# LayerNorm at the start of a spectral block plus MLP kernel: four groups of four token tiles instead of five groups of two and four, first scaling on Pool, first tables issued from the ACT queue

## The chip, the cores and the metric

The kernel runs on one core of a Trainium2 chip. The metric is device time in microseconds (us) of one execution; the kernel before takes 502.8 us. The profiled span is about 2 us shorter than the device time of the same execution.

Names: PE is the matrix engine, DVE the vector engine, ACT the scalar engine, Pool the GPSIMD engine, SP the engine that here issues most DMA transfers.

## The reference

The change touches only the first LayerNorm, without scale and offset, whose result goes into a two-dimensional Fourier transform.

```python
def _layernorm(x, axis=-1, eps=1e-5):
    m = jnp.mean(x, axis=axis, keepdims=True)
    v = jnp.var(x, axis=axis, keepdims=True)
    return (x - m) / jnp.sqrt(v + eps)

def _A_ref(x, w_r, w_i):                     # x: 1 x 2048 x 576, bf16
    X = rfft2(x.astype(float32)) * (w_r + 1j * w_i)
    return irfft2(X, s=(2048, 576)).astype(bfloat16)

h  = x + _A_ref(_layernorm(x), A_w_r, A_w_i)
h2 = h + ((gelu(LN(h) @ w_gate) * (LN(h) @ w_up)) @ w_down)     # the MLP
```

## The kernel before

The 2048 tokens lie in 16 tiles of 128. The sequence transform's first stage multiplies a tile (as weights) by a table of 128 columns. LayerNorm's factor 1/sqrt(var + eps) is one number per token, so the kernel scales the *table* with it (`ATS = ATB * RS1`) and never the tile. Variances are worked out for a group of tiles at once, and the five groups run as a pipeline:

1. statistics of each tile: on DVE two `bn_stats` and one `bn_aggr` (`ln1_tile`), or, for the tiles in `ACT_TILES`, sum and sum of squares on ACT (`act_sum`, `act_sq`) and two one-column steps on DVE;
2. square root on ACT, reciprocal on DVE;
3. table scaling, on DVE (four instructions of 128 columns) or Pool (one of 512);
4. matmuls on PE, five outputs k of each group;
5. evictions, that is copies, of the five results from PSUM (the memory that PE writes to) into `U` on ACT or DVE (`a_evs`).

When all of `U` is there, the forward DFT over the columns starts (`st_D`, "PS<-FT,U"), then the spectral stage (`st_B`, "PS<-CUS,BT").

```python
    P.op(POOL, lambda g: g.memset(EPT[:, :], EPS), w=["EPT"])
    # ... more memsets on Pool
    x_load(0, 0, 2)            # all on the SP queue; x_load(i, c0, c1) = tiles c0..c1-1
    x_load(1, 2, 4)
    atb_load(0, 0, 4)          # table columns of tiles 0 to 3
    x_load(2, 4, 8)
    atb_load(1, 4, 8)
    x_load(3, 8, 12)
    x_load(4, 12, 16)
    atb_load(2, 8, 16)
    # [cut]
    GROUPS = ((0, 2), (2, 4), (4, 8), (8, 12), (12, 16))
    ACT_TILES = (1, 3, 7, 11, 13)

    def ln1_var(i):
        c0, c1 = GROUPS[i]
        for c in range(c0, c1):
            if c in ACT_TILES:         # TM = sum^2 / D^2: one column, both inputs in SBUF
                P.op(DVE, lambda v, c=c: v.scalar_tensor_tensor(TM[:, 0, c:c + 1], SA[:, 0, c:c + 1], 1.0 / (D * D), SA[:, 0, c:c + 1],
                                                                op0=ALU.mult, op1=ALU.mult), r=[("SA0", c)], w=[("TM", c)])
            else:
                P.op(DVE, lambda v, c=c: v.bn_aggr(MV1[:, c, :], ST1[:, c, :, :]), r=[...], w=[("MV1", c)])
        for c in range(c0, c1):
            if c in ACT_TILES:         # variance = squares / D - TM
                P.op(DVE, lambda v, c=c: v.scalar_tensor_tensor(MV1[:, c, 1:2], SA[:, 1, c:c + 1], 1.0 / D, TM[:, 0, c:c + 1],
                                                                op0=ALU.mult, op1=ALU.subtract), r=[...], w=[("MV1", c)])

    def ln1_scale(i, eng):
        c0, c1 = GROUPS[i]
        if eng == POOL:
            P.op(POOL, lambda g, c0=c0, c1=c1: g.tensor_tensor(ATS[:, c0:c1, :], ATB[:, c0:c1, :],
                 RS1[:, c0:c1].unsqueeze(2).to_broadcast([128, c1 - c0, 128]), op=ALU.mult), r=[...], w=[...])
        else:
            for c in range(c0, c1):
                P.op(DVE, lambda v, c=c: v.tensor_scalar(ATS[:, c, :], ATB[:, c, :], RS1[:, c:c + 1], None, op0=ALU.mult), r=[...], w=[...])

    def idle_mm(n, i):     # n matmuls of zeros, to keep PE busy while it has nothing to do
        ...
    # the order of issue, group by group [cut to its start]
    idle_mm(11, 0)
    act_sum(1); act_sq(1)
    ln1_tile(0); ln1_tile(2)
    act_sum(3)
    ln1_var(0); ln1_sqrt(0)
    act_sq(3)
    ln1_rs(0); ln1_scale(0, DVE); a_mms(0)
    ln1_var(1); ln1_sqrt(1)
    a_evs(0, ACT, (0, 1, 2, 3, 4))
    ln1_rs(1); ln1_scale(1, DVE)
    idle_mm(2, 1)
    a_mms(1)
    ln1_tile(4); ln1_tile(5); ln1_tile(6)
    # [cut: groups 2, 3 and 4]
```

## Time and profile before

| | value |
|---|---|
| device time, median of 3 | 502.81 us (502.74 to 503.13) |
| profiled span | 501.2 us |
| PE busy, whole span | 98% |
| start of tile 4's statistics on DVE | 8.22 us |
| first forward-DFT matmul | 20.17 us |

First, lines of the page of the kernel before: the engines' busy times, and the clock granted to PE in 40 slices of 12.5 us.

```profile
PE 492.9 (98%) x4319; PEld 299.5 (60%) x4319; DVE 182.5 (36%) x391; ACT 158.4 (32%) x296; POOL 39.8 (8%) x49
...
PE   7999999999999999999999999999999999999998
...
PEclk9899999999999999999999999999999999999999
```

PE has idle time to lose only in the first slice (7 tenths) and in the last (8 tenths, which the change does not touch), and a lower clock mainly in the second (8 tenths). The change lies in these two slices, and it can gain or lose only by moving the moment at which the forward DFT starts. Next the chain of waits of the kernel before, that is, the work that ended last, followed back. The columns are start, duration and what ran.

```profile
2.12 6.08 DMA XO<-in_A_x_dram
...
8.22 2.26 DVE ST L440 x6
...
17.65 0.58 DVE ATS L472 x3
18.23 1.80 DVE U L505 x3
20.04 0.14 issue
20.17 2.55 PE PS L600 x18
22.72 0.52 PE PS L626 x6
```

It starts with the x transfer for tiles 4 to 7, issued at 2.12 and landed at 8.2. From then on DVE works almost without a gap to its last eviction, and the forward DFT starts at 20.17.

DVE scales tables for group 1 until about 8.1, so an x that lands earlier than that would find DVE busy. And the one-column step of tile 13 (line 446, at 16.04) takes 0.11 us.

Last, two rows of the busy-by-window view of the kernel before: busy time and instruction count per engine, the mean granted clock, and the DMA share.

```profile
core 0: us, PE busy (x) PEld busy (x) DVE busy (x) ACT busy (x) POOL busy (x), PEclk, DMA share, GB/s
...
13.70:17.10 3.40, 3.40 (x21) 2.12 (x22) 3.40 (x15) 3.40 (x10) 1.04 (x1) 0.50 1.10 228
```

PE ran at half clock from 13.7 to 17.1, and ACT was as busy as DVE there.

### The profile page before, as it was taken

How to read it: one execution, taken by the hardware profiler on the slowest of the kernel's cores; microseconds unless marked ns; L12 is line 12 of the kernel's file. 1: busy time of each engine (PE TensorE's matmuls, PEld its weight loads, DVE VectorE, ACT ScalarE, POOL GpSimd, SP SyncE). 2: the span in 40 equal slices, each digit the busy share in tenths (PEclk: the TensorE clock that was granted, in tenths of full speed). 3: DMA queues.
4: the chain of work that ended last, by engine and by line, in shares of the span. 5: the costliest groups of instructions: out<-in, count | busy, mean ns of one | idle time of the engine just before them, and what ended most of it. 6: DMA issues, size and time to landing. Idle time of an engine off the chain costs nothing.

```text
span 501.2 us, 9972 instructions
## 1 busy us (share of the span) xinstructions
PE 492.9 (98%) x4319; PEld 299.5 (60%) x4319; DVE 182.5 (36%) x391; ACT 158.4 (32%) x296; POOL 39.8 (8%) x49
## 2 busy tenths in 40 slices
PE   7999999999999999999999999999999999999998
PEld 2687674444457764444477744444677544444775
DVE  5899663344331114433311044433201233333111
ACT  7888766653220012332300023232100123233000
POOL 3645290000000000000000000000000000000000
PEclk9899999999999999999999999999999999999999
DMA  8769989001100000100000001100000000000000
GB/s 280 168 203 327 313 288 319 2 7 25 26 1 19 18 13 20 22 14 1 2 12 13 19 18 21 24 2 1 1 18 19 13 1 1 1 2 1 13 19 19
DMA packets 25948, 28.64 MB, mean 57 GB/s; under 512 B 11568, under 2 KB 19888, under 8 KB 25776
## 3 DMA queue, kind: packets, MB, share of 16 engines
q1 hardware_dynamic: 23328, 17.39, 12.1%
q0 software_dynamic: 2576, 10.62, 6.3%
q8 instruction: 34, 0.56, 0.5%
q14 instruction: 10, 0.08, 0.1%
HBM read 23.66 MB, written 2.36 MB: 52 GB/s over the span
## 4 chain that ended last, share of the span: by engine, by line
PE 90%; DVE 7%; issue 1%; DMA 1%; SPq 0%; ACT 0%; DVEq 0%
PE PS L861 56%; PE PS L884 28%; PE PS L723 3%; DVE TP L635 2%; PE PS L762 2%; DVE ST L440 1%; DMA XO<-in_A_x_dram 1%; DVE ZS L640 1%; DVE CUS L613 1%; PE PS L600 1%; DVE U L505 0%; SPq L206 0%; PE PS L807 0%; PE PS L654 0%; DVE CUS L610 0%
## 5 line engine op out<-in xcount | busy, mean ns | idle before, releaser
L861 PE MATMUL PS<-HT,WGU 64*128 64x512 bf16 x2592 | 281.9, 376 | 0.0
L861 PEld LDWEIGHTS PS<-HT,WGU 64*128 64x128 bf16 x2592 | 137.9, 94 | 142.8 <-issue 1.2
L873 ACT ACTIVATE GL<-PS 128x512 bf16<-128x512 f32 x144 | 85.9, 597 | 289.3 <-PE PS L861 288.5
L874 DVE TENSOR_TENSOR AT<-GL,PS 128x512 bf16<-128x512 bf16 x144 | 98.9, 688 | 174.2 <-PE PS L861 172.5
L884 PE MATMUL PS<-WD,AT 128*128 128x288 bf16 (+2 forms) x1152 | 141.8, 286 | 0.0
L884 PEld LDWEIGHTS PS<-WD,AT 128*128 128x128 bf16 x1152 | 111.0, 98 | 31.5 <-issue 1.7
L887 DVE TENSOR_TENSOR OS<-PS,XO 128x288 bf16<-128x288 f32 (+2 forms) x32 | 14.6, 458 | 125.8 <-PE PS L884 125.8
L674 POOL TENSOR_SCALAR WS<-WS 128x290 bf16<-128x290 bf16 x16 | 15.9, 996 | 9.6 <-DMA WS<-in_A_w_i_dram 5.9
L765 DVE SCALAR_TENSOR_TENSOR XO<-PS,XO 128x576 bf16<-128x576 f32 x16 | 12.1, 756 | 8.4 <-PE PS L762 8.4
L600 PE MATMUL PS<-FT,U 128*128 128x290 bf16 x96 | 14.4, 287 | 0.4 <-DVE U L505 0.4
L723 PE MATMUL PS<-DT,V 128*128 128x289 bf16 x96 | 14.6, 287 | 0.2 <-DVE V L660 0.2
L635 DVE TENSOR_TENSOR TP<-YS,WS 128x580 bf16<-128x580 bf16 (+2 forms) x34 | 14.1, 453 | 0.3 <-issue 0.3
L654 PE MATMUL PS<-VT,ZS 128*128 128x256 bf16 x96 | 13.1, 272 | 1.0 <-DVE ZS L640 1.0
L665 ACT ACTIVATE V<-PS 128x768 bf16<-128x768 f32 x15 | 12.2, 810 | 1.2 <-PE PS L654 1.0
L629 ACT ACTIVATE YS<-PS 128x578 bf16<-128x578 f32 x16 | 10.5, 654 | 3.3 <-PE PS L626 2.9
L732 ACT ACTIVATE GS<-PS 128x578 bf16<-128x578 f32 x15 | 9.8, 654 | 4.2 <-PE PS L723 4.1
L723 PEld LDWEIGHTS PS<-DT,V 128*128 128x128 bf16 x96 | 8.9, 97 | 3.5 <-issue 0.4
L600 PEld LDWEIGHTS PS<-FT,U 128*128 128x128 bf16 x96 | 9.2, 98 | 2.9 <-issue 0.6
L753 ACT ACTIVATE OS<-XO 128x576 bf16<-128x576 bf16 x16 | 10.8, 674 | 0.0
L626 PE MATMUL PS<-CUS,BT 128*128 128x289 bf16 (+2 forms) x96 | 10.7, 247 | 0.0
L762 PE MATMUL PS<-GS,IT 128*128 128x288 bf16 x64 | 10.5, 285 | 0.0
L483 PE MATMUL PS<-ZD 128*128 128x512 bf16 x24 | 9.1, 537 | 1.3 <-POOL ZD L377 1.3
(58 smaller groups left out, 156.6 us busy)
## 6 DMA issues: line engine op xcount, KB each, us to landing
WD<-in_B_w_down_dram POOLq DMA_DIRECT2D x9, 576.0 KB, 8.4
WGU<-in_B_w_up_dram SPq DMA_DIRECT2D x4, 1152.0 KB, 9.7
WGU<-in_B_w_gate_dram POOLq DMA_DIRECT2D x4, 1152.0 KB, 10.3
out_dram<-OS SPq DMA_DIRECT2D x30, 72.0 KB, 1.6
XO<-in_A_x_dram SPq DMA_DIRECT2D x3, 576.0 KB, 7.6
IT<-c_itab SPq DMA_DIRECT2D x1, 1024.0 KB, 7.0
HT<-HN SPq DMA_TRANSPOSE x60, 2.4
XO<-in_A_x_dram SPq DMA_DIRECT2D x2, 288.0 KB, 3.1
```

What stands on the lines that cost most here:

```text
L600: P.op(PE, lambda t, b=b, o=o, dt=dt, us=us, g=g: t.matmul(bank(b, 0, 128, 0, 2 * HK), U[:, us, g, :, :], FT[:, o, dt, :], start=(dt == 0) ...
L635: P.op(DVE, lambda v: v.tensor_tensor(TP[:, sl, t_, :, q0:q1], YS[:, sl, :, q0:q1], WS[:, g, w_, q0:q1], op=ALU.mult), r=[("Y", sl), ("Wn" ...
L654: P.op(PE, lambda t, b=b, o=o, c=c, zp=zp, sl=sl, sp_=sp_: t.matmul(bank(b, 0, 128, o, o + 256), ZS[:, sl, zp, 128 * c:128 * c + 128], VT[ ...
L665: P.op(ACT, lambda a, g=g, src=src: a.activation(V[:, :, :, g, :], src, ACTF.Copy), r=[("PS", bs[0]), ("PS", bs[2]), "Vfree"], w=[("V", g, ...
L674: P.op(POOL, lambda v, g=GORD[i]: v.tensor_scalar(WS[:, g, 0, :], WS[:, g, 2, :], -1.0, None, op0=ALU.mult), r=[k for k in wkeys[0 if 1 <= ...
L723: P.op(PE, lambda t, b=b, h=h, i=i, kt=kt, c=c: t.matmul(bank(b, 0, 128, 0, K2), V[:, kt, c, :, :], DT[:, 3 * h + i, 0:K2], start=(i == 0) ...
L762: P.op(PE, lambda t, b=b, h=h, i=i, c=c, rhs=rhs: t.matmul(bank(b, 0, 128, 0, 288), IT[:, h * i, c, :], rhs, start=(i == 0), stop=(i == 1) ...
L861: op = P.op(PE, lambda t, h0=h0, kt=kt, wt=wt, f=f, b=b, HT=HT, s=(half == 0 and j in (0, 5)), e=(half == 1 and j in (3, 8)): t.matmul(ban ...
L873: P.op(ACT, lambda a, s2=s2, b0=b0: a.activation(GL[:, s2, :], bank(b0), ACTF.Gelu_apprx_tanh), r=[("PS", b0)], w=[("GL", s2)])
L874: P.op(DVE, lambda v, s2=s2, b0=b0, f=f: v.tensor_tensor(AT[:, f, :], GL[:, s2, :], bank(b0 + 1), op=ALU.mult), r=[("GL", s2), ("PS", b0 + ...
L884: P.op(PE, lambda t, b=b, d0=d0, d1=d1, f=f, p=p: t.matmul(bank(b, 0, 128, 0, d1 - d0), AT[:, f, 128 * p:128 * p + 128], WD[:, f, d0:d1], ...
L887: P.op(DVE, lambda v, b=b, d0=d0, d1=d1, p=p, c=c: v.tensor_tensor(OS[:, p % 2, d0:d1], bank(b, 0, 128, 0, d1 - d0), XO[:, c, d0:d1], op=A ...
```

## The change

The intent: two small groups cost DVE two rounds of small steps and four table scalings before tile 4 can start. One group of four tiles, three on DVE and one on ACT, with its table scaled by Pool, should let DVE start on tile 4 as soon as x arrives; and with the first table loads moved to ACT's queue, x should be issued earlier. A tiny multiply on Pool is meant to bring the loading of Pool's library forward to where nothing waits for it.

```diff
     P.op(POOL, lambda g: g.memset(EPT[:, :], EPS), w=["EPT"])
+    P.op(POOL, lambda g: g.tensor_tensor(RS2[:, 0:1], EPT[:, :], EPT[:, :], op=ALU.mult), r=["EPT"], w=[("V2", 0)])
 ...
     x_load(0, 0, 2)
     x_load(1, 2, 4)
-    atb_load(0, 0, 4)
     x_load(2, 4, 8)
-    atb_load(1, 4, 8)
     x_load(3, 8, 12)
     x_load(4, 12, 16)
     atb_load(2, 8, 16)
 ...
-    GROUPS = ((0, 2), (2, 4), (4, 8), (8, 12), (12, 16))
-    ACT_TILES = (1, 3, 7, 11, 13)
+    GROUPS = ((0, 4), (4, 8), (8, 12), (12, 16))
+    ACT_TILES = (1, 7, 11, 13)
 ...
-    idle_mm(11, 0)
+    atb_load(0, 0, 4, ACT)
+    atb_load(1, 4, 8, ACT)
+    idle_mm(17, 0)
 ...            # the new order; group 0 scaled by Pool, group 3 by DVE. Its part from group 1 on:
+    ln1_rs(1)
+    ln1_scale(1, POOL)
+    idle_mm(5, 1)
+    a_mms(1)
 ...
+    ln1_var(2)
+    a_evs(1, ACT, (0,))
+    ln1_sqrt(2)
+    act_sum(13)
+    act_sq(13)
+    ln1_tile(14)
+    ln1_rs(2)
+    ln1_scale(2, POOL)
+    ln1_tile(15)
+    a_evs(1, ACT, (1,))
+    ln1_var(3)
+    a_evs(1, DVE, (4,))
+    ln1_sqrt(3)
+    a_evs(1, ACT, (2, 3))
+    idle_mm(4, 2)
+    a_mms(2)
```

More of the change, by code (lines that the diff above doesn't have):

```diff
@@ L385, in x_load, with atb_load @@
         P.dma(SP, XO[:, c0:c1, 0:D], xv[:, c0:c1, :], f"x{i}", w=[("X", c) for c in range(c0, c1)])
-    def atb_load(i, c0, c1):
-        P.dma(SP, ATB[:, c0:c1, :], tabs[:, c0:c1, :], f"atb{i}", w=[("ATB", c) for c in range(c0, c1)])
+    def atb_load(i, c0, c1, eng=SP):
+        P.dma(eng, ATB[:, c0:c1, :], tabs[:, c0:c1, :], f"atb{i}", w=[("ATB", c) for c in range(c0, c1)])
     x_load(0, 0, 2)
     x_load(1, 2, 4)
-    atb_load(0, 0, 4)
     x_load(2, 4, 8)
-    atb_load(1, 4, 8)
     x_load(3, 8, 12)
@@ L522, in _build @@
     ln1_tile(2)
-    act_sum(3)
+    ln1_tile(3)
     ln1_var(0)
     ln1_sqrt(0)
-    act_sq(3)
     ln1_rs(0)
-    ln1_scale(0, DVE)
+    ln1_scale(0, POOL)
     a_mms(0)
-    ln1_var(1)
-    ln1_sqrt(1)
-    a_evs(0, ACT, (0, 1, 2, 3, 4))
-    ln1_rs(1)
-    ln1_scale(1, DVE)
-    idle_mm(2, 1)
-    a_mms(1)
     ln1_tile(4)
@@ L541, in _build @@
     act_sq(7)
-    a_evs(1, ACT, (0, 1))
+    a_evs(0, ACT, (0, 1, 2))
+    ln1_var(1)
+    ln1_sqrt(1)
+    a_evs(0, ACT, (3, 4))
+    ln1_tile(8)
+    ln1_rs(1)
+    ln1_scale(1, POOL)
+    idle_mm(5, 1)
+    a_mms(1)
+    ln1_tile(9)
+    ln1_tile(10)
+    ln1_tile(12)
+    act_sum(11)
+    act_sq(11)
     ln1_var(2)
+    a_evs(1, ACT, (0,))
     ln1_sqrt(2)
-    a_evs(1, ACT, (2, 3, 4))
-    ln1_tile(8)
+    act_sum(13)
+    act_sq(13)
+    ln1_tile(14)
     ln1_rs(2)
     ln1_scale(2, POOL)
-    idle_mm(7, 2)
-    a_mms(2)
-    act_sum(11)
-    act_sq(11)
-    ln1_tile(9)
-    ln1_tile(10)
-    act_sum(13)
-    ln1_var(3)
-    ln1_sqrt(3)
-    act_sq(13)
-    ln1_tile(12)
-    ln1_rs(3)
-    ln1_scale(3, POOL)
-    ln1_tile(14)
-    a_evs(2, ACT, (0, 1, 2))
-    ln1_tile(15)
-    ln1_var(4)
-    a_evs(2, DVE, (4,))
-    ln1_sqrt(4)
-    ln1_rs(4)
-    ln1_scale(4, DVE)
-    a_evs(2, ACT, (3,))
-    idle_mm(4, 3)
-    a_mms(3)
-    a_evs(3, ACT, (0,))
-    a_evs(3, DVE, (1,))
-    a_evs(3, ACT, (2,))
-    a_evs(3, DVE, (3,))
-    a_evs(3, ACT, (4,))
-    a_mms(4)
-    a_evs(4, DVE, (0,))
-    a_evs(4, ACT, (1,))
-    a_evs(4, ACT, (2,))
-    a_evs(4, DVE, (3,))
-    a_evs(4, ACT, (4,))
+    ln1_tile(15)
[5 more added lines that the diff above has]
+    idle_mm(4, 2)
+    a_mms(2)
+    ln1_rs(3)
+    ln1_scale(3, DVE)
+    a_evs(2, ACT, (0, 1))
+    a_evs(2, DVE, (2, 3))
+    a_evs(2, ACT, (4,))
+    a_mms(3)
+    a_evs(3, ACT, (0, 1))
+    a_evs(3, DVE, (2,))
+    a_evs(3, ACT, (3,))
+    a_evs(3, DVE, (4,))
     uk = [[("U", i, k) for i in range(len(GROUPS))] + ["Uz"] for k in range(5)]
```

## The prediction

> **What bounds the kernel now.** The page gives PE 98% of the 501.2 us span, but the change touches only the first 20 us. The chain of waits there runs: x transfer for tiles 4 to 7 (lands at 8.2), then DVE without a gap (statistics, reciprocals, table scaling, evictions) until the first forward-DFT matmul (L600) at 20.17. After that the spectral stage is DVE-bound (32.2 of 33.5 us busy, busy-by-window view) and then PE-bound, so a shift of the 20.17 start should reach the end about one to one. ACT is just as full: the timeline shows it busy from 12.04 to 20.47 without a gap over 0.2 us.
>
> **What the change removes, adds, moves.**
> - Groups of two tiles (0-1, 2-3) become one of four. Before tile 4 can start, DVE drops four table scalings (0.17 us apart) and one set of small variance steps, and gains two statistics (0.37 each). DVE should be done with group 0 at 7.0 rather than 8.14. After tile 4 its work is nearly the same (scalings 4, evictions 5, statistics alike).
> - ACT loses one tile's two sums (1.35 us), but before 8 us, where it waits for x anyway. After 8.7 us it has ten-plus evictions of 512 columns (0.48 us apart) in place of five of 256 (0.26): some 1 us more.
> - The two small table loads leave the SP queue, so x for tiles 4-7 is issued at about 1.65 instead of 2.11 and x for 8-15 0.9 earlier. The Trainium skill (DMA: Bandwidth & Descriptors, "Issuing engines are not separate DMA queues") says that only issue time is saved; the trace agrees that the engines are near saturation from 5 us. I expect tiles 4-7 at 7.3 to 8.0, and the first table at about 6.5.
> - The first scaling goes to Pool: one 1.04 us instruction, result at about 8.2, so matmuls of group 0 from 8.3.
> - The tiny Pool multiply pulls the Pool library configuration (in the trace at 4.43 us, behind the memsets, hidden in a wait of 7.3 us) to 1.45 us, ahead of memsets worth 3.0 us. The skill (GPSIMD Engine Reference, "Instruction dispatch") gives about 6 us for a first call after such a load. This trace bounds it only from above: under 7.3 us.
>
> **Sum.** Laying the measured durations in program order gives (my estimate): with a load under 3 us, last eviction 0.0 to 0.7 us earlier; break-even near 3.3 us; with 6 us Pool runs configuration to 7.4, memsets to 10.9, the scaling at 11, group-0 evictions on ACT at 12.5, and the second square root, behind those in ACT's order, at 14 instead of 11.05. DVE then sits at the reciprocal for some 2.7 us, and the end moves by 2.5 to 2.9 us. I give the long load somewhat over half. The weight loads that wait for the second memset are delayed about 1 us, with about 4 us of slack.
>
> **Predicted: 504.0 us**, range 502.0 to 506.0. Faster by over 2%: 0.003; within 2%: 0.992; slower: 0.005.
>
> **What would show it.** Right: a gap on Pool of several us after 1.45 before the tiny multiply; the first scaling at 10 or later; a DVE wait of over 1 us at the second reciprocal; L600 starting at 21.5 to 23. Wrong: scaling at 7.2 to 7.6, group-0 matmuls at 8.3, no DVE gap, L600 at 19.5 to 20.2 and a time of 502.2. The half-speed clock seen at 13.7 to 17.1 should vanish in that case.
>
> **What would make it wrong.** A short or already resident library; x landing later because two queues interleave; ACT rather than DVE ending last; slack downstream that swallows the shift.

## More of the kernel before

On the timeline of DVE in the kernel before one can see what it did just before tile 4. The number in brackets would be an idle time and what ended it; there is none at 8.22.

```profile
7.52 0.17 DVE L462 RECIPROCAL RS<-RS 128x2 f32<-128x2 f32 x1 [0.36 <-ACT RS L457]
7.72 0.42 DVE L472 TENSOR_SCALAR ATS<-ATB,RS 128x128 bf16<-128x128 bf16 x2
8.22 2.26 DVE L440 BATCH_NORM_STATS2 ST<-XO 128x6 f32<-128x288 bf16 x6
...
16.04 0.11 DVE L446 SCALAR_TENSOR_TENSOR TM<-SA 128x1 f32<-128x1 f32 x1
```

## The result, and the profile after

| | before | after |
|---|---|---|
| device time, median of 4 | 502.77 us (502.59 to 503.13) | 503.30 us (502.65 to 503.51) |
| ratio after/before | | 1.0007, 95% interval 0.9990 to 1.0025 |
| profiled span | 501.2 us | 501.2 us |

The outputs are correct. A ratio is the mean time of one kernel's fast runs over that of the other's fast runs of the same rounds, so it is not quite the ratio of the medians quoted. The two kernels take the same time within what these runs can tell. This is within the predicted range, but the sum that led to 504.0 did not come about, as the profile shows. The page of the kernel after hardly differs from the page before.

```profile
PE 492.8 (98%) x4320; PEld 299.5 (60%) x4321; DVE 182.3 (36%) x387; ACT 156.4 (31%) x286; POOL 40.7 (8%) x51
...
PEclk9899999999999999999999999999999999999999
```

**The library load.** The timeline of Pool in the kernel after:

```profile
1.30 0.10 POOL L378 MEMSET EPT<- 128x1 f32 x1
1.49 0.19 POOL L379 TENSOR_TENSOR RS<-EPT 128x1 f32<-128x1 f32 x1
...
7.24 1.04 POOL L466 TENSOR_TENSOR ATS<-ATB,RS 128x512 bf16<-128x512 bf16 x1 [2.48 <-DVE RS L461]
11.77 1.04 POOL L466 TENSOR_TENSOR ATS<-ATB,RS 128x512 bf16<-128x512 bf16 x1 [3.49 <-DVE RS L461]
15.25 1.04 POOL L466 TENSOR_TENSOR ATS<-ATB,RS 128x512 bf16<-128x512 bf16 x1 [2.45 <-DVE RS L461]
```

There is no gap of several us before the tiny multiply. The first real scaling starts at 7.24 and was waiting for DVE's reciprocal, which ended at 7.1. The raw instruction records (not a view of the profile; start in us, duration in ns) also name the configuration instructions, which the timeline leaves out:

```
after:   1.342  11 MODIFY_POOL_CONFIG
         1.372  11 MODIFY_POOL_CONFIG
         1.483 192 TENSOR_TENSOR RS<-EPT
before:  4.425  11 MODIFY_POOL_CONFIG
         4.455  11 MODIFY_POOL_CONFIG
         4.514 7346 EVENT_SEMAPHORE        (a wait)
        11.965 1037 TENSOR_TENSOR ATS<-ATB,RS
```

From the second configuration record to the first multiply it is 0.11 us. Before, the same would have been hidden in a wait of 7.35 us, which is why that trace could only bound it from above.

**The start of tile 4.** The timeline of DVE in the kernel after:

```profile
6.92 0.18 DVE L461 RECIPROCAL RS<-RS 128x4 f32<-128x4 f32 x1 [0.36 <-ACT RS L456]
8.02 2.26 DVE L439 BATCH_NORM_STATS2 ST<-XO 128x6 f32<-128x288 bf16 x6 [0.92 <-DMA XO<-in_A_x_dram]
...
15.84 0.47 DVE L445 SCALAR_TENSOR_TENSOR TM<-SA 128x1 f32<-128x1 f32 x1
```

DVE is free at 7.1, as planned, and then waits 0.92 us for the x of tiles 4 to 7, although its transfer was issued 0.48 us earlier than before (1.64 against 2.12). Note also the last line: the one-column step takes 0.47 us in place of 0.11.

**The end of the stage.** The chain of waits of the kernel after:

```profile
1.64 6.36 DMA XO<-in_A_x_dram
...
8.02 2.26 DVE ST L439 x6
...
15.92 0.39 DVE TM L445
...
16.61 0.30 ACT RS L456
16.91 3.85 ACT U L506 x8
20.75 0.05 issue
20.80 2.04 PE PS L591 x15
22.84 0.51 PE PS L617 x6
```

ACT now ends last, with eight evictions in a row to 20.75. (A few first DFT matmuls start at 20.05 and then wait for that eviction.) Measured from the start of tile 4, the first spectral matmul (PS<-CUS,BT) comes after 22.84 − 8.02 = 14.82 us; before, it was 22.72 − 8.22 = 14.50. So the kernel after starts tile 4 a little earlier and takes longer from there. The timeline of ACT in the kernel after says where it waits:

```profile
14.34 0.30 ACT L456 ACTIVATE RS<-MV,EPT 128x4 f32<-128x4 f32 x1 [0.41 <-DVE MV L451]
...
16.61 0.30 ACT L456 ACTIVATE RS<-MV,EPT 128x4 f32<-128x4 f32 x1 [0.16 <-DVE MV L451]
16.81 3.93 ACT L506 ACTIVATE U<-PS 64x512 bf16<-64x512 f32 x8
```

ACT idles twice in front of a square root (line 456), because DVE's variance is not there yet, while evictions that it could do stand behind in its order. It also has more of them: after 8.7 us its evictions sum to 7.7 us in this timeline (15 of 512 columns), and to 6.9 us before (10 of 512 and 5 of 256).

**The half clock.** Two rows of the busy-by-window view of the kernel after (columns as above):

```profile
6.90:13.70 6.80, 4.24 (x40) 2.49 (x39) 5.75 (x22) 5.68 (x15) 2.08 (x2) 0.97 1.05 390
13.70:17.10 3.40, 3.18 (x23) 2.05 (x21) 3.30 (x18) 2.83 (x9) 1.04 (x1) 0.55 1.15 224
```

In this execution the half clock did not vanish; the records put it at 13.35 to 16.76. (The other three executions of the kernel after had a granted clock of 1.0; this one had 0.997.) The timeline of PE in the kernel after shows PE idle before group 1's matmuls, and the last forty table matmuls, which matter in e8:

```profile
12.86 2.15 PE L493 MATMUL PS<-ATS,XO 128*128 128x128 bf16 x20 [1.93 <-POOL ATS L466]
...
16.51 3.01 PE L493 MATMUL PS<-ATS,XO 128*128 128x128 bf16 x40
```

**The theory after this look, and its rivals.** Theory: (1) the library load is about 0.1 us and plays no part. (2) The chain starts at the landing of x for tiles 4 to 7, which the order of issue hardly moves and which differs from execution to execution; the new grouping only makes DVE free early enough to use an early landing. (3) This small gain is given back between tile 4 and the DFT, by a port lock between Pool and DVE at tile 13 and by ACT's order. Rivals: the load is long but hidden by luck; the earlier issue does bring x earlier and something else eats it; the half clock costs the time; or the end does not feel a shift of the first stage at all.

### The profile page after: what moved, and what is told of

It is laid out like the page before. It is cut to its first block, busy times and chain, and to the rows that moved or that the text cites. A ratio compares the mean times of both kernels' runs of the same rounds, so it can differ in the third digit from the quotient of the medians.

```text
span 501.2 us, 9961 instructions
## 1 busy us (share of the span) xinstructions
PE 492.8 (98%) x4320; PEld 299.5 (60%) x4321; DVE 182.3 (36%) x387; ACT 156.4 (31%) x286; POOL 40.7 (8%) x51
## 4 chain that ended last, share of the span: by engine, by line
PE 90%; DVE 6%; DMA 1%; issue 1%; ACT 1%; SPq 0%; DVEq 0%
PE PS L852 56%; PE PS L875 28%; PE PS L714 3%; DVE TP L626 2%; PE PS L753 2%; DVE ST L439 1%; DMA XO<-in_A_x_dram 1%; DVE ZS L631 1%; ACT U L506 1%; PE PS L591 1%; DVE CUS L604 1%; PE PS L798 0%; PE PS L645 0%; PE PS L617 0%; DVE CUS L601 0%
## 5 line engine op out<-in xcount | busy, mean ns | idle before, releaser
L439 DVE BATCH_NORM_STATS2 ST<-XO 128x6 f32<-128x288 bf16 x24 | 9.2, 445 | 4.7 <-DMA XO<-in_A_x_dram 4.7
```

The costliest lines, as they stand in the source:

```text
L439: P.op(DVE, lambda v, c=c, h=h: v.bn_stats(ST1[:, c, h, :], XO[:, c, 288 * h:288 * h + 288]), r=[("X", c)], w=[("ST1", c, h)])
```

## Experiments

In the table, t4 is the start of tile 4's statistics. "Half clock" is how long PE's granted clock stood at one half. All distances come from the instruction records of one profiled execution of each kernel.

| profiled execution | t4 | t4 to first spectral matmul | t4 to end | end | half clock |
|---|---|---|---|---|---|
| before | 8.21 | 14.35 | 492.98 | 501.20 | 3.4 |
| before again | 8.05 | 14.35 | 492.90 | 500.94 | 3.4 |
| e6_dma_only | 9.50 | 14.36 | 492.90 | 502.40 | none |
| after | 8.02 | 14.66 | 493.21 | 501.22 | 3.4 |
| e1_no_warm | 7.29 | 14.67 | 493.40 | 500.69 | none |
| e3_sum_first | 8.54 | 14.67 | 493.19 | 501.73 | 3.4 |
| e5_warm_pe | 7.63 | 14.67 | 493.21 | 500.85 | none |
| e7_dma_undone | 7.60 | 14.67 | 493.20 | 500.80 | none |
| e2_one_input | 8.21 | 16.05 | 494.75 | 502.96 | 6.8 |
| e4_delay | 8.04 | 17.13 | 495.66 | 503.71 | 6.8 |
| e8_no_idle | 7.13 | 15.93 | 494.65 | 501.78 | 10.2 |
| e11_order_port | 7.21 | 14.04 | 492.52 | 499.73 | none |
| e9_combined | 7.93 | 14.04 | 492.50 | 500.43 | none |
| e12_split_x | 6.92 | 14.56 | 493.26 | 500.17 | none |

(The records and the chain differ by up to 0.16 us in the start of that matmul, the same way in both kernels.) Three groups of rows repeat to about 0.01 us in the distance from t4 to the first spectral matmul: 14.35 with the old schedule, 14.67 with the new one, 14.04 with the repaired one. e12 stands apart, because its chain no longer starts at tile 4.

### e1_no_warm: the kernel after without the tiny multiply

```diff
-    P.op(POOL, lambda g: g.tensor_tensor(RS2[:, 0:1], EPT[:, :], EPT[:, :], op=ALU.mult), r=["EPT"], w=[("V2", 0)])
```

> The changed kernel without the tiny Pool multiply, so that the Pool library configuration falls behind the memsets again (about 4.5 us). The prediction's theory (a load of about 6 us after the configuration): first scaling at 10.5 us or later, first L600-type matmul (forward DFT) at 22 us or later, time 2 us longer than the changed kernel. Rival (the trace of the changed kernel: the multiply starts 0.1 us after the configuration): first scaling at 7.2 us, forward DFT at 20.0, time equal to the changed kernel's within 0.3 us.

Measured: 502.95 us (502.63 to 503.26), ratio to before 1.0008 (0.9992 to 1.0025). In the records the configuration is back at 4.43 and 4.46 us, and the first scaling starts at 7.205, on time for the reciprocal. A load of 6 us from 4.46 would have held it until 10.4. So the load has no cost to see wherever it stands, and the multiply that was to hide it does nothing. Whether a load took place at all, or the code was already in Pool's memory from an earlier execution, these runs do not settle. The DMA records speak against a load inside the span: in the profiles of before, after and e1, no packet of the kind "instruction" starts between 0 and 18.4 us. A load by a way that the profiler does not record is not excluded.

### e2_one_input: both one-column steps with a single tensor input

```diff
-  v.scalar_tensor_tensor(TM[:, 0, c:c + 1], SA[:, 0, c:c + 1], 1.0 / (D * D), SA[:, 0, c:c + 1],
+  v.tensor_scalar(TM[:, 0, c:c + 1], SA[:, 0, c:c + 1], SA[:, 0, c:c + 1], 1.0 / (D * D),
-  v.scalar_tensor_tensor(MV1[:, c, 1:2], SA[:, 1, c:c + 1], 1.0 / D, TM[:, 0, c:c + 1],
+  v.tensor_scalar(MV1[:, c, 1:2], SA[:, 1, c:c + 1], 1.0 / D, TM[:, 0, c:c + 1],
```

> The two one-column variance steps of ACT-summed tiles rewritten with one tensor input and a pointer scalar instead of two tensor inputs. In the changed kernel the step of tile 13 takes 0.47 us (0.10 elsewhere) and ends when Pool's third scaling ends (16.29). Theory port lock: the step takes 0.10 again, the third square root on the variance chain starts 0.2 to 0.3 us earlier (16.35), last evictions end 0.2 to 0.3 us earlier, forward DFT about 19.8. Rival (it waits for ACT's sum, or for something else): the step still ends near 16.3. Either way the time differs by under 0.4 us from the changed kernel.

The Trainium skill (SBUF — State Buffer, "Who interferes with whom") says that a DVE instruction with two SBUF inputs contends with a Pool instruction that reads SBUF, and that the loser waits for the whole instruction. In the kernel after the step started at 15.84, inside Pool's scaling of 15.25 to 16.29, and ended with it. The timeline of DVE in this experiment:

```profile
16.25 0.16 DVE L445 TENSOR_SCALAR TM<-SA 128x1 f32<-128x1 f32 x1
```

And the timeline of Pool in this experiment:

```profile
15.66 1.04 POOL L466 TENSOR_TENSOR ATS<-ATB,RS 128x512 bf16<-128x512 bf16 x1 [2.56 <-DVE RS L461]
```

The step falls inside Pool's 15.66 to 16.70 again, and takes 0.16 us instead of 0.47. This trace agrees with the page: the lock is shown, and it cost 0.47 − 0.11 = 0.36 us. The records of the other new-schedule profiles say the same: in all seven that keep the two-tensor form (after, e1, e3, e4, e5, e7, e8) tile 13's step takes 0.47 us and ends within 0.02 us of Pool's scaling, and the same step outside a scaling takes 0.10 or 0.11.

The form with one tensor costs 0.05 us more per step where there is no conflict, and I had used it in all groups. That ate the gain. Counted from tile 4, the square root of group 2 started 6.54 us later here and 6.32 in the kernel after, and the last one 8.56 and 8.59. The last square root on the timeline of ACT in this experiment:

```profile
16.77 0.30 ACT L456 ACTIVATE RS<-MV,EPT 128x4 f32<-128x4 f32 x1
```

The time did not follow: 503.22 us (502.21 to 504.92), ratio 1.0015 (0.9995 to 1.0036), and the first DFT matmul, at 21.61, missed my expectation. So this run did not test the removal of the lock by itself. The profiled execution also had two half-clock windows in a row (14.76 to 21.59), in which the last forty table matmuls took 4.95 us; in the kernel after they took 3.01. This led to e5 and e8.

### e3_sum_first: ACT sums tile 13 before it takes the square root of group 2

```diff
-    ln1_sqrt(2)
     act_sum(13)
+    ln1_sqrt(2)
     act_sq(13)
```

> ACT does the sum of tile 13 before the square root of group 2 instead of after it. Theory that ACT is what ends the stage in the changed kernel and that its 0.5 us idle before that square root is lost work: ACT's last eviction ends 0.3 to 0.5 us earlier than 20.74, while the square root starts 0.15 later, and the forward DFT matmuls end up to 0.3 us earlier. Rival (DVE alone sets the end): DVE's last eviction moves 0.15 later and the DFT with it.

Measured: 503.25 us (502.56 to 503.78), ratio 1.0012 (0.9997 to 1.0027). The first wait did go: the timeline of ACT in this experiment has no bracket at the square root at 15.00. But another one grew at the next:

```profile
15.00 0.30 ACT L456 ACTIVATE RS<-MV,EPT 128x4 f32<-128x4 f32 x1
...
17.13 0.30 ACT L456 ACTIVATE RS<-MV,EPT 128x4 f32<-128x4 f32 x1 [0.69 <-DVE MV L451]
```

The last square root starts 17.13 − 8.54 = 8.59 us after tile 4, exactly as in the kernel after (16.61 − 8.02). It waits for DVE, and DVE was held by the port lock. My expectation of 0.3 to 0.5 us was wrong: two waits stand in a row, and removing the first alone only lengthens the second.

### e4_delay: six extra statistics on DVE before tile 4

```diff
+    for _ in range(3):
+        ln1_tile(4)
```

> Six useless statistics instructions on DVE (the statistics of tile 4 three times over; the result is the same), 2.16 us, just as x for tile 4 lands. Theory that the chain from there to the end of the kernel is tight: the forward DFT starts 2.1 us later and the whole time is 2.0 to 2.3 us longer. Rival (slack downstream or in the stage swallows a shift): the DFT starts 2.1 later, but the end moves by under 1.2 us.

Measured: 505.22 us (504.56 to 505.82), ratio 1.0051 (1.0036 to 1.0066). The added work is 2.16 us of DVE; from tile 4 to the end the profile grows by 495.66 − 493.21 = 2.45 us, of which a second half-clock window can have a part. The end does feel a shift of this stage, about one to one. The same can be read without any edit: in the rows after, e3, e5 and e7 of the table, t4 differs by 0.94 us and t4-to-end by 0.02. (e1 is 0.2 us longer. The records put this between the first spectral matmul and the start of the MLP, which comes 67.23 us after tile 4 and 67.04 in the kernel after; the reason was not looked for.)

### e5_warm_pe: eleven matmuls of zeros instead of five before group 1

```diff
-    idle_mm(5, 1)
+    idle_mm(11, 1)
```

> Eleven instead of five idle matmuls ahead of group 1, so that TensorE is not idle for 2.3 us there. Theory that the half clock seen after that gap costs time only when it lasts two stretches (6.8 us, as in two of the last four profiles, where the forward DFT began 13.4 and 14.75 us after the first statistics of tile 4 instead of 12.0, the second with 2.2 us of added work): no half clock in the profile, the DFT 12.0 us after tile 4's statistics, no execution over 503.6, median 0.2 to 0.5 us below the changed kernel. Rival (the clock doesn't matter here, matmuls are not what the stage waits for): same spread and median as the changed kernel, 503.3.

Measured: 502.86 us (502.58 to 503.42), ratio 1.0004 (0.9990 to 1.0018). All five executions had a granted clock of 1.0 throughout. Yet t4-to-end is 493.21, the same as in the kernel after with one half-clock window. So one such window, in the place where it fell, costs nothing; removing it is only a guard against a second.

### e8_no_idle: no matmuls of zeros in the middle of the stage

```diff
-    idle_mm(5, 1)
 ...
-    idle_mm(4, 2)
```

> The changed kernel without the nine idle matmuls ahead of groups 1 and 2 (the seventeen at the start stay). Theory that the TensorE clock is what varies between executions: half clock for two stretches (6.8 us) in the profile and in most executions, the forward DFT 13.2 us or more after tile 4's statistics, median at 504.0 to 505. Rival (the clock doesn't matter): 503.3, DFT at 12.0.

Measured: 503.88 us (503.70 to 504.56), just under the 504.0 to 505 that I expected, ratio 1.0024 (1.0011 to 1.0036). By their granted clocks of 0.990 to 0.993 every execution had two or three half-clock windows (one window makes 0.997). Three rows of its busy-by-window view (columns as above):

```profile
6.90:13.70 6.80, 3.23 (x34) 2.51 (x35) 6.54 (x27) 6.19 (x17) 2.08 (x2) 0.81 1.04 390
13.70:17.10 3.40, 2.48 (x22) 1.85 (x21) 3.29 (x16) 3.24 (x10) 1.04 (x1) 0.50 1.16 225
17.10:20.50 3.40, 3.40 (x29) 2.83 (x30) 2.05 (x5) 2.89 (x6) 2.87 (x3) 0.50 0.51 105
```

And the last forty table matmuls on the timeline of PE in this experiment:

```profile
15.47 4.95 PE L493 MATMUL PS<-ATS,XO 128*128 128x128 bf16 x40 [0.92 <-POOL ATS L466]
```

Here the half clock lasts to 21.4 and covers all of these matmuls, and again they take 4.95 us. That puts t4-to-end at 494.65, or 1.4 us more than in the kernel after. So the half clock costs something when it covers those last forty matmuls, and nothing was seen of it where it ended before them or early in them (in e10 it reached from 14.04 to 17.46, over the first part of matmuls that ran from 16.12 to 19.57, and the distance to the end, 492.90, equals that of e6, which had no half clock). In all these traces its length is 3.413 us, or two or three times that; the Trainium skill (TensorE: Matmul & The Clock Gate, "Part 1: The HAM clock gate") gives a free-running window of 3413 ns, and this agrees.

### e6_dma_only and e7_dma_undone: the issue of the tables on its own

e6 is the kernel before with the first two table loads on ACT's queue; e7 is the kernel after with them back on SP in their old places.

```diff
 e6:  -    atb_load(0, 0, 4)                 e7:  +    atb_load(0, 0, 4)
      -    atb_load(1, 4, 8)                      +    atb_load(1, 4, 8)
      +    atb_load(0, 0, 4, ACT)                 -    atb_load(0, 0, 4, ACT)
      +    atb_load(1, 4, 8, ACT)                 -    atb_load(1, 4, 8, ACT)
```

> The kernel before with only the two small table loads moved to the ACT queue. Theory: x for tiles 8 to 15 lands about 1.2 us earlier (9.4 and 10.9), x for tiles 4 to 7 between 7.3 and 8.5 as in the five profiles that have this order; but DVE is busy with the small groups to 8.1, so tile 4 starts at 8.15 at the earliest, and the time equals that of the kernel before within 0.3 us. Rival (the transfers were all the gain): tile 4 starts earlier than 8.0, and the time falls by 0.3 us or more.

> The changed kernel with the table loads back on the SP queue in their old places. Theory: x for tiles 4 to 7 lands at 8.2 as in the kernel before, tile 4 starts then, and because the new schedule needs 0.1 to 0.3 us more from there to the end, the time is 0.1 to 0.4 us above the kernel before and 0.2 above the changed one. Rival (landing times are set by chance and not by this order): x for tiles 4 to 7 lands anywhere in 7.3 to 8.5, and the time equals that of the changed kernel.

Measured: e6 503.22 us (503.12 to 504.20), ratio 1.0014 (1.0002 to 1.0027); e7 502.86 us (502.36 to 503.37), ratio 1.0001 (0.9989 to 1.0014). The timeline of DVE in e6 shows something that I had expected in neither theory:

```profile
7.79 0.42 DVE L470 TENSOR_SCALAR ATS<-ATB,RS 128x128 bf16<-128x128 bf16 x2 [1.14 <-DMA ATB<-c_atab]
```

In this execution the first table landed only at 7.76 us, DVE waited 1.14 us for it, and tile 4 started at 9.50, 1.3 us later than in the kernel before. In the kernel after the first table landed at 5.25, in e8 at 6.05, and before, on SP, at 5.87. Both expectations for e6 failed: its median is 0.4 us above before, neither within 0.3 nor lower. In e7 x for tiles 4 to 7 landed at 7.58 and not at the expected 8.2, so there the rival on the landing was right. On its own the move to ACT's queue is a small loss in the old schedule (the interval of the ratio lies above 1); that a late first table also explains the four executions without a trace is not shown.

The landing of x for tiles 4 to 7, which the move was to bring forward, over all profiles with one of these two orders (e9, with the second table on SP, had 7.91):

| order of issue | landing of x for tiles 4 to 7, us | mean |
|---|---|---|
| tables on SP, x issued at 2.1 (before, before again, e7) | 8.19, 7.42, 7.58 | 7.73 |
| tables on ACT, x issued at 1.6 (after, e1, e2, e3, e4, e5, e8, e11, e6) | 7.99, 7.27, 8.18, 8.51, 8.02, 7.61, 7.11, 7.19, 7.99 | 7.76 |

An issue 0.48 us earlier brought no earlier landing that could be seen against a spread of 1.4 us. The later transfers do move: x for tiles 12 to 15 landed at 12.09 and 11.26 in the two profiles of before and at 10.22 to 11.32 with the new order, but nothing waits for them. This agrees with the Trainium skill (DMA: Bandwidth & Descriptors, "Issuing engines are not separate DMA queues"): only the time of issue is saved. Why the landing varies these runs do not say.

### e10_before_again: the kernel before, unchanged

> The kernel before, unchanged, as a null comparison and for a second profile. Theory that x for tiles 4 to 7 lands by chance between 7.1 and 8.5 and that the kernel before can't use an early landing because DVE is busy with its second small group to 8.1: tile 4's statistics start at 8.1 or later whatever the landing, the forward DFT 11.9 to 12.0 after that, and the time differs from the kernel before by under 0.15 us. Rival (landing follows the order of issue): x for tiles 4 to 7 at 8.2 again.

Measured: 502.63 us (502.51 to 502.87), ratio 0.9998 (0.9985 to 1.0010). This is the width of the method, and it gave by chance the case that I needed: an early landing, at 7.42. The timeline of DVE in this execution:

```profile
7.72 0.42 DVE L472 TENSOR_SCALAR ATS<-ATB,RS 128x128 bf16<-128x128 bf16 x2
8.05 2.25 DVE L440 BATCH_NORM_STATS2 ST<-XO 128x6 f32<-128x288 bf16 x6
```

Tile 4 starts at 8.05 all the same, after the small groups' scalings. So in this execution the kernel before got at most 0.17 us (8.05 against 8.22) from a landing 0.77 us earlier. The kernel after can use more: with the new grouping and the new issue the mean of t4 over eight profiles is 7.76, against 8.21 and 8.05 in the two profiles of before. In these profiles that is a gain of 0.4 us, but eight values that spread from 7.13 to 8.54 against two leave it uncertain by about 0.2.

The spans of the executions without a trace make it smaller. The mean span of 39 executions of before is 500.88 us, and of 22 of the new schedule (after, e1, e3, e5, e7) 501.00. If the distances from tile 4 to the end (492.94 and 493.24 on average in the profiles) hold for those as well, then the mean t4 is 7.94 before and 7.76 after. This is my estimate: a gain of about 0.2 us, with the two profiles of before on the late side. The device times add something that no view shows: the device time exceeds the span by 1.85 us on average in 44 executions of before and e6, and by 2.03 in 50 of the kernel after and its variants. Thus some 0.17 us of what the kernel after loses lies outside the profiled span, and its cause is open.

It also fits that the times of the kernel before scatter less (502.4 to 503.1 over all rounds) than those of the new schedule (502.4 to 503.8 over after, e1, e3, e5 and e7).

### e11_order_port: both repairs together

The kernel after with the one-tensor form for tile 13 alone, `act_sum(13)` before the square root, and one eviction of group 1 moved forward in ACT's order.

```diff
-            if c in ACT_TILES:
+            if c == 13:
+                (the two steps as tensor_scalar, as in e2)
+            elif c in ACT_TILES:
 ...
-    ln1_sqrt(2)
     act_sum(13)
+    ln1_sqrt(2)
 ...
-    a_evs(1, ACT, (1,))
+    a_evs(1, ACT, (1, 2))
     ln1_var(3)
 ...
-    a_evs(1, ACT, (2, 3))
+    a_evs(1, ACT, (3,))
```

> The repairs on ACT's order and of tile 13's variance steps alone; idle matmuls and transfers as in the changed kernel. Theory: the forward DFT 11.6 to 11.8 us after tile 4's statistics where the half clock lasts one stretch or none, 1 us or more later where it lasts two; time 0.2 to 0.4 us below the changed kernel (503.3), so about 502.9. Rival (ACT's idle time and the port wait don't matter): 12.0 and 503.3.

Measured: 502.77 us (501.69 to 503.38), ratio 0.9995 (0.9983 to 1.0008). From tile 4 to the first spectral matmul it is 14.04 us instead of 14.67, and to the end 492.52 instead of 493.21. The last square root on the timeline of ACT in this experiment has no wait in front of it:

```profile
15.58 0.31 ACT L462 ACTIVATE RS<-MV,EPT 128x4 f32<-128x4 f32 x1
```

Counted from tile 4 it starts at 8.36 us instead of 8.59, and seven evictions follow it on ACT instead of eight (3.50 us instead of 3.93). So the repairs together were worth 0.7 us, though moving the sum alone was worth nothing in e3, and the one-tensor form alone, used in all groups in e2, lost on the way what it gained. The repair of tile 13's step alone was not run. Against before that distance is now 0.4 us shorter. The device times scatter over 1.7 us. The two longest (503.06 and 503.38) had one half-clock window and the others none; whether it covered the last forty table matmuls or x landed late in them is not on record, since only the profiled execution, one of the two fastest, has a trace.

### e9_combined: e11, the eleven matmuls of e5, and the second table load on SP

```diff
     x_load(3, 8, 12)
+    atb_load(1, 4, 8)
     x_load(4, 12, 16)
 ...
-    atb_load(1, 4, 8, ACT)
-    idle_mm(5, 1)
+    idle_mm(11, 1)
     (and the edits of e11)
```

> The changed kernel with four repairs: eleven idle matmuls ahead of group 1 (no half clock), tile 13's two variance steps with one tensor input (not held up by Pool's scaling), tile 13's sum ahead of the square root of group 2 and one more eviction ahead of the last square root (no idle on ACT), and the second table piece on the SP queue between x for tiles 8 to 11 and 12 to 15 (not beside x for tiles 4 to 7). Theory that these are what the changed kernel loses after tile 4 starts: the forward DFT 11.6 to 11.8 us after tile 4's statistics (12.0 in the changed kernel, 11.96 before), from there to the end 492.6 to 492.9 us (493.2; 493.0 before), x for tiles 4 to 7 at 7.0 to 8.0, time 0.4 to 0.9 us below the kernel before, ratio 0.9982 to 0.9992. Rival (the time is set later, or by chance alone): ratio 1.000 or more.

Measured: 502.38 us (501.68 to 502.50), before in the same rounds 502.83 (502.57 to 502.89), ratio 0.9989 (0.9975 to 1.0003). All clocks were 1.0. Since the distance to the end equals that of e11 (492.50 and 492.52), the two further repairs show no gain of their own in the profile. Its highest run is below the lowest of nine runs of before, but the interval of the ratio includes 1.

### e12_split_x: e9 with x for tiles 4 to 7 as two loads

```diff
-    x_load(2, 4, 8)
+    x_load(2, 4, 6)
+    x_load(5, 6, 8)
```

> The kernel with the four repairs, with x for tiles 4 to 7 loaded by two transfers of two tiles instead of one of four. Theory that the landing of x for tile 4 is what starts the chain: tiles 4 and 5 land at 6.0 to 6.8, their statistics start at 7.1 (when DVE has the first reciprocal behind it) instead of 7.9, the forward DFT 11.7 to 11.9 us after that, the time 0.4 to 0.9 us below the kernel with the four repairs, ratio to the kernel before 0.997 to 0.9985. Rival (DVE then waits for tiles 6 and 7, or ACT for tile 7): tile 4 starts at 7.1 but the forward DFT stays at 19.5 or later, and the time equals that of the four repairs within 0.2 us.

Measured: 502.11 us (501.83 to 502.37), before in the same rounds 502.73 (502.53 to 502.85), ratio 0.9989 (0.9975 to 1.0003). Tiles 4 and 5 landed at 6.67, and tile 4 started at 6.92, as soon as DVE was free. But the forward DFT came 12.29 us after that and not 11.7 to 11.9, and the ratio missed the expected 0.997 to 0.9985. The chain of waits of this kernel has a new start:

```profile
2.12 5.49 DMA XO<-in_A_x_dram
...
7.63 0.78 ACT JNK L432 x2
...
9.08 1.44 ACT U L514 x3
10.52 0.19 ACT RS L464
...
19.21 2.43 PE PS L598 x18
```

It now begins with tiles 6 and 7, and runs over ACT: tile 7's sums cannot start before 7.63, three evictions stand before the square root of group 1, and DVE waits for that. So part of the rival came true (ACT is late with tile 7), though the DFT moved. The forward DFT starts at 19.21, which is 0.96 us earlier than in the profile of before, and the span is 500.2 against 501.2 (on average over the executions of these rounds, 500.1 against 500.8). It is the best version by median (0.6 us under before), still well within 2%, and with an interval of the ratio that just includes 1.

## Why the prediction was right or wrong

The time, 503.30, lies in the range of 502 to 506, and "within 2%" came out. That is partly luck: the range of 4 us was wide enough for both branches of the prediction, so landing in it says little about the mechanism. The central figure of 504.0 rested on a step that failed.

- **Failed: "with 6 us Pool runs configuration to 7.4", "the scaling at 11", "and the end moves by 2.5 to 2.9 us".** The prediction gave this branch somewhat over half, from the skill's figure of about 6 us for a first call (GPSIMD Engine Reference, "2.1 Instruction dispatch"). The runs show 0.11 us between configuration and multiply, the first scaling at 7.24, and no delay in e1 either. The end did not move: the span is 501.2 in both.
- **The other branch had its marks on the trace right, but not its direction.** The prediction asked for a scaling at 7.2 to 7.6 (7.24), group-0 matmuls at 8.3 (8.33 on the timeline of PE), and no DVE gap at the second reciprocal (there is none). It gave "last eviction 0.0 to 0.7 us earlier" and 502.2; the last eviction ended 0.1 us later (20.74 against 20.62), and the time was 503.3.
- **What its sum left out.** The port lock on tile 13's step, 0.36 us of DVE (e2), and ACT's order with its waits before two square roots (e3, e11). Their repair together gave 0.7 us. The prediction counted ACT's added evictions, at 1 us (7.7 against 6.9 us in the timelines), and named "ACT rather than DVE ending last" as a way to be wrong, but did not lay ACT's order against DVE's.
- **"I expect tiles 4-7 at 7.3 to 8.0" from an issue 0.5 us earlier.** The landing of 7.99 fits, but the reason does not: both orders have nearly the same mean (7.73 and 7.76), and single executions spread from 7.1 to 8.5.
- **Right: DVE done with group 0 at 7.0** (7.10), and through this tile 4 starts earlier, by 0.4 us in the profiles and by about 0.2 by the estimate from all spans. The distance from there to the end is 0.2 to 0.3 us longer (493.20 against 492.90 to 492.98). Gain and loss nearly cancel, and the measured ratio of 1.0007 with its interval of ±0.0017, or about 0.9 us, is consistent with that and cannot resolve it.
- **Right: "a shift of the 20.17 start should reach the end about one to one"** (e4, and the constant t4-to-end distances).
- **Wrong: the half clock "should vanish".** In the profiled execution, though not in the other three, it stayed, at 13.35 to 16.76, after PE had idled 1.93 us before group 1's matmuls. With that gap filled it was gone in all five executions (e5). It cost nothing in that place, but 1.4 us where it covered the last forty table matmuls (e8).

Still open: whether Pool's code was already resident; why the kernel after has 0.17 us more outside its profiled span; why the same transfer lands between 7.1 and 8.5 us; and whether the kernel after is slower or faster than before by a few tenths of a microsecond.

## What to carry to other kernels

When a large rearrangement moves the time little, measure distances between two events of one execution: here the end minus the start of tile 4 repeated to 0.02 us in four profiles of five, while whole times scattered by 1 us, and that separated a gain of a few tenths at tile 4 from a loss of 0.3 behind it. But a few profiles are a small sample of where an execution starts: check them against the times of all executions. Freeing an engine early is worth only as much as the transfer that it then waits for allows. And where two engines hand work to each other, look for a second wait behind the one that you remove: moving ACT's sum alone gave nothing, and with the repair of DVE's step and one eviction moved as well it gave 0.7 us.

## What the Trainium skill lacked or had wrong

- GPSIMD Engine Reference, "2.1 Instruction dispatch": about 6 us for the first call to a freshly loaded kernel, counted from the configuration record. Here it is 0.11 us from the second configuration record (1.372) to the multiply (1.483), and a scaling at 7.205 was on time after a configuration at 4.46. The page doesn't say how to tell from a program or a trace whether a call needs a load; whether the code was resident was not tested.
- SBUF — State Buffer, "Who interferes with whom": agrees, but gives no size for tiny instructions. A one-column DVE step took 0.47 us instead of 0.11 because it fell inside a Pool instruction of 1.04 us. The page's way out, at most one SBUF input, comes without an example: here the same arithmetic with one tensor and a per-partition scalar took 0.16 us inside Pool's instruction.
- TensorE: Matmul & The Clock Gate, "Part 1: The HAM clock gate": the window of 3413 ns agrees with the lengths of 3.413, 6.827 and 10.24 us. The page's table puts the half clock after at least one idle window of about 3.4 us; here it followed an idle time of 1.93 us with work on both sides (the kernel after), the same kernel's other executions had none (granted clock 1.0 in three of four), and in e6 an idle time of 2.28 us before the matmuls of the same tiles brought none.
- DMA: Bandwidth & Descriptors: no word on how far the landing of the same transfer spreads between executions. Here a load of 576 KB issued at 1.6 us landed between 7.1 and 8.5 us, and the first table on ACT's queue between 5.19 and 7.76 us.
